# A routed feed-forward kernel: the third and fourth tile of an expert's tokens as one pair of 256 tokens, other PSUM banks in the branches, branch hints later in a tile, and the pair's code last in its branch

## The chip, the cores and the metric

The program runs on one core of one Trainium2 chip. The metric is the device time of one execution in microseconds; shown is the median of several. A core has five engines with their own instruction queues: TensorE (PE, matmuls; PEld are its weight loads), VectorE (DVE), ScalarE (ACT), GpSimd (POOL) and SyncE (SP, which here only starts transfers). They meet by semaphores.

## The reference

Three stages follow each other. Local and global attention of 4 batches and 8 heads gives 2176 tokens of width 512. Each goes through a feed-forward layer (512 to 2048, squared ReLU, back to 512). Then comes the stage that is changed here, a layer of 8 experts:

```python
skip_score = x @ w_skip
do_compute = skip_score > 0
out = x.copy()
xc = x[do_compute]
logits = xc @ w_gate
e_idx = np.argmax(logits, axis=1)
gate_w = ...                        # the softmax probability of the chosen expert
for e in range(E):
    mask = e_idx == e
    h = np.maximum(xc[mask] @ w1[e], 0.0)       # 512 to 1024
    y[mask] = gate_w[mask, None] * (h @ w2[e])  # 1024 to 512
out[do_compute] = xc + y
```

How many tokens an expert gets depends on the data: the program learns it while it runs.

## The kernel before

The order of all work is written out by hand. For the experts it is plain program order: expert 0 to 7, and within an expert tiles of 128 tokens, tile 0 always and each later one in a runtime branch, nested: `more(e, j)` is an `If` on the expert's count of tokens that holds tile `j` and, inside, `more(e, j + 1)`; after tile 4 comes a loop. An engine that skips such an arm runs a few instructions in its place that wait until the engine's own work is done and then raise the semaphores by what the arm would have raised them. They have the line of the `If` (L1166). L1151 marks a branch hint: each engine is told early which way the branch will go.

Products are made at near float32 precision: each operand is split into a high and a low part, and a product is three matmuls (high by high, high by low, low by high). A tile (`expert_tile`) gathers its 128 token rows by an indirect transfer (L863, into `xg`), transposes them on PE (`etr`, four 128x128 transposes), and splits the result on ACT and DVE (`prepare`, `xp`). The first product (L889 to L891) has the tokens as the stationary operand and 512 columns of w1 as the moving one, so its result `eh` has tokens on the partitions; ACT applies ReLU (L894), PE transposes `er` back (`ertr`, four transposes for each half of the 1024 columns), ACT and DVE split that (`ehl`), and the second product (L904 to L906) adds up `y` over 8 blocks. DVE multiplies by the gate and adds the token (`eo`, L927), and POOL scatters the rows to the output (L931).

A tile is a generator of nine units u = 0 to 8. Beside them the program places the gathers of later tiles, the transposes of the next tile (u = 5 in tile `j` for tile `j + 1`; in tile 0 also u = 6 for the next expert), and, in tile 0 only, the conversion of an expert's weights: eight pieces of 512 KB, each cast to its high part on ACT (L828, `e26h` for piece 26, which is expert 3's third) and subtracted for the low part on DVE (L834, `e26l`). The pieces of an expert are converted from u = 3 of the tile before into its own tile 0. The first results `eh` of all tiles go to the PSUM tag "h" with two banks; the tags "s" and "o" with one bank each served the attention and are free here.

Of the kernel before, what the change touches and what calls it, by code (L numbers as in the profile page):

```python
# [53 lines left out]
def attention_ffn_routed_experts(  # L54
# [25 lines left out]
    P = 128  # L80
# [96 lines left out]
    def split(hi, lo, src, lo_engine=None):  # L177

        nc.scalar.copy(hi, src)  # L179
        (lo_engine or nc.vector).tensor_tensor(out=lo, in0=src, in1=hi.bitcast(F32), op=ALU.subtract)  # L180
# [625 lines left out]
    AHEAD = {2: ((2, 0),), 3: ((1, 1),)}  # L806
    PARTS_AT = {0: (0, 1), 1: (2,), 2: (3,), 3: (4,), 4: (5,), 5: (6,), 6: (7,)}
    U0, U1 = 6, 5

    def fetch_expert(n, queue=nc.sync):  # L810
        e, i = divmod(n, NPE)
# [42 lines left out]
                xps[chain, z] = sb(tag, bufs, [P, 2, KD, P], f"xp{chain}_{z}", F32R)  # L854

    def gathered(e, j):
        return xgs[(0, e % 3) if j == 0 else (1, e % 2) if j % 2 else (2, 0)]

    def prepared(e, j):
        return xps[(0, e % 2) if j == 0 else (1, 0) if j == 1 else (2, j % 2)]  # L860

    def gather(e, j, gi):
        nc.gpsimd.indirect_dma_start(  # L863
# [4 lines left out]
    def prepare(e, j):  # L868
        tr = pair(f"etr_{e}_{j}")
        transposes(tr, gathered(e, j))  # L870
        x = prepared(e, j)
        split(x[:, 0], x[:, 1], tr)

    def expert_tile(e, j, si):

        name = f"{e}_{j}"
        xg, p = gathered(e, j), prepared(e, j)
        hs, rs = [None] * 2, [None] * 2
        hl = sb("kT", 1, [P, NPAIR, S], f"ehl_{name}").rearrange("p a s -> p (a s)")[:, 0:2 * KE * P].bitcast(F32R)
        gh, gl = (hl[:, z * KE * P:(z + 1) * KE * P].rearrange("p (f k) -> p f k", f=KE) for z in range(2))  # L880
        y = ps.tile([P, DM], F32, tag="x2", bufs=2, name=f"y_{name}")

        def first(fb, k0, k1):
            if k0 == 0:
                hs[fb] = ps.tile([P, 512], F32, tag="h", bufs=2, name=f"eh_{name}_{fb}")
            h = hs[fb]
            for k in range(k0, k1):
                wh, wl = ew[e, 1, (fb, k)]
                nc.tensor.matmul(h, lhsT=p[:, 0, k, :], rhs=wh, start=(k == 0), stop=False)  # L889
                nc.tensor.matmul(h, lhsT=p[:, 0, k, :], rhs=wl, start=False, stop=False)  # L890
                nc.tensor.matmul(h, lhsT=p[:, 1, k, :], rhs=wh, start=False, stop=(k == KD - 1))  # L891
            if k1 == KD:
                rs[fb] = sb("sm", 2, [P, S], f"er_{name}_{fb}")[:, 0:512]
                nc.scalar.activation(rs[fb], h, AF.Relu)  # L894

        def turn(fb):
            tr = pair(f"ertr_{name}_{fb}")
            transposes(tr, rs[fb])
            split(gh[:, 4 * fb:4 * fb + 4, :], gl[:, 4 * fb:4 * fb + 4, :], tr)

        def second(f0, f1):
            for f in range(f0, f1):
                wh, wl = ew[e, 2, f]
# [12 lines left out]
        yield  # L916
        second(0, 2)
        turn(1)
        yield
        second(2, 4)  # L920
        yield
        second(4, 6)
        yield
        second(6, KE)
        yield
        o = sb("xt", 1, [P, 3 * BLK], f"eo_{name}")[:, 0:DM]
        nc.vector.scalar_tensor_tensor(  # L927
            out=o, in0=y, scalar=xg[:, DM:DM + 1], in1=xg[:, 0:DM], op0=ALU.mult, op1=ALU.add
        )
        yield  # L930
        nc.gpsimd.indirect_dma_start(  # L931
            out=out, out_offset=bass.IndirectOffsetOnAxis(ap=si, axis=0), in_=o, in_offset=None,
            bounds_check=NTOK - 1, oob_is_err=False,
        )

    rest = []

    def prepare_rest():
# [6 lines left out]
    def rest_tile(si):  # L945

        e, x, fw = E - 1, rest[0], F // NQ
        xg = gathered(e, 1)[0:SEG]
        raws = [est[e * NPE + i] for i in range(NPE)]
        h = ps.tile([P, 512], F32, tag="h", bufs=2, name="eh_rest")[:, 0:fw]  # L950
        for k in range(KD):
            for c in range(NQ):
                fb, at = divmod(c * fw, DM)
                nc.tensor.matmul(
                    h[SEG * c:SEG * (c + 1), :], lhsT=x[:, k, :],
                    rhs=raws[fb * (KD // 2) + k // 2][:, k % 2, at:at + fw],
                    start=(k == 0), stop=(k == KD - 1),
                )
        r = sb("sm", 2, [P, S], "er_rest")[:, 0:fw]
        nc.scalar.activation(r, h, AF.Relu)  # L960
        tr = pair("ertr_rest")
        nz = fw // P
# [13 lines left out]
        o = sb("xt", 1, [P, 3 * BLK], "eo_rest")[0:SEG, 0:DM]  # L976
        for d in range(NQ):
            cols = slice(d * P, (d + 1) * P)
            nc.vector.scalar_tensor_tensor(
                out=o[:, cols], in0=y[SEG * d:SEG * (d + 1), :], scalar=xg[:, DM:DM + 1], in1=xg[:, cols],  # L980
                op0=ALU.mult, op1=ALU.add,
            )
        nc.gpsimd.indirect_dma_start(  # L983
            out=out, out_offset=bass.IndirectOffsetOnAxis(ap=si[0:SEG], axis=0), in_=o, in_offset=None,
            bounds_check=NTOK - 1, oob_is_err=False,
        )
# [4 lines left out]
    with tc.manual_schedule():  # L991
# [103 lines left out]
        def slot(idx, e, j):  # L1095
            c = e * TPE + j
            return idx[:, c:c + 1]
# [46 lines left out]
                gather(n, j, slot(gidx, n, j))  # L1144

        def least(e, j):
            return j * P + (SEG if (e, j) == (E - 1, 1) else 0)

        def hint(e, j):

            tc.mark_branch_hint_location(f"more{e}_{j}", hint=n_tok[e] > least(e, j), engines=ENGINES)  # L1151

        def more(e, j):

            if j == UNROLL:
                with tc.For_i(UNROLL, (n_tok[e] + (P - 1)) // P, 1) as it:
                    gi = sb("gi", 2, [P, 1], f"gi{e}", I32)
                    nc.vector.tensor_copy(gi, gidx[:, bass.ds(it + e * TPE, 1)])
                    si = sb("si", 2, [P, 1], f"si{e}", I32)
                    nc.vector.tensor_copy(si, sidx[:, bass.ds(it + e * TPE, 1)])  # L1160
                    gather(e, UNROLL, gi)
                    prepare(e, UNROLL)
                    for _ in expert_tile(e, UNROLL, si):
                        pass
                return
            with tc.If(n_tok[e] > least(e, j), label=f"more{e}_{j}") as branch:  # L1166
                if j + 1 < UNROLL:
                    hint(e, j + 1)
                    gather(e, j + 1, slot(gidx, e, j + 1))
                for u, _ in enumerate(expert_tile(e, j, slot(sidx, e, j))):  # L1170
                    if u == 5 and j + 1 < UNROLL:
                        prepare(e, j + 1)
                more(e, j + 1)
            if least(e, j) > j * P:
                with branch.Else():
                    with tc.If(n_tok[e] > j * P):
                        rest_tile(slot(sidx, e, j))

        n_tok = None
        for e in range(E):  # L1180
            for u, _ in enumerate(expert_tile(e, 0, slot(sidx, e, 0)) if e else ()):
                if u == 0:
                    hint(e, 1)
                if u == U1:
                    prepare(e, 1)
                    if e == E - 1:
                        prepare_rest()
                if u == U0 and e + 1 < E:
                    prepare(e + 1, 0)
                work(e, u)  # L1190
# [39 lines left out]
```

## Time and profile before

| | |
|---|---|
| runs | 741.7, 740.62, 739.76 us; median 740.62 us |
| the profiled execution | 740.43 us, of which the span from first to last instruction is 738.6 us |
| PE busy over the span | 708.3 us (96%), 7509 matmuls |
| DVE, ACT, POOL busy | 420.2, 393.3, 168.5 us |
| mean granted TensorE clock | 0.988 of 2.4 GHz |

The experts' tiles stand from about 557 us to the end. Experts 0 and 3 have several full tiles, expert 7 one and a small rest, the others one tile each. Matmuls overlap, so the distance between the starts of two of them is the time that one costs, not its duration; a start that is later than its predecessor's by more than that distance is a wait. In the rows "[0.27 <-ACTq L1166]" is the idle time before an instruction and what ended it; a q behind an engine's name means its instruction queue, not its data path.

### The profile page before, as it was taken

To read this page: it belongs to the slowest core of one execution; us is meant where nothing else is said; L and a number is where in the kernel's file an instruction comes from. 1 tells how busy PE (TensorE), PEld (TensorE's weight loads), DVE (VectorE), ACT (ScalarE), POOL (GpSimd) and SP (SyncE) were. 2 spreads that over 40 slices of the span, in tenths; PEclk is the share of its full clock that TensorE was granted. 3 is DMA by queue.
4 is the path that set the end of the run, shared out by engine and by line. 5 is a ranking of instruction groups with operands and counts; after the bars stand their busy time and mean duration, and the time that the engine had idled before them with its cause. 6 is when DMAs were issued, how large, how long until landed. Compare 5 with 4: busy or idle time off the path is not lost. (4 is left out here: it accounts for less than half of the span.)

```text
span 738.6 us, 18687 instructions
## 1 busy us (share of the span) xinstructions
PE 708.3 (96%) x7509; PEld 588.1 (80%) x7509; DVE 420.2 (57%) x1077; ACT 393.3 (53%) x968; POOL 168.5 (23%) x213
## 2 busy tenths in 40 slices
PE   6689999999999999999999999999999999999996
PEld 4466677889888888888888988888878777887774
DVE  1889955853652463556165265342576279615993
ACT  5767567665544553534555454343354368515781
POOL 5000144461121121212112111122132222222121
PEclk8799999999999999999999999999999999999999
DMA  9999461073146114063501204100475779615920
GB/s 269 249 296 302 173 152 36 19 182 47 35 107 145 48 37 105 2 133 77 123 31 37 70 14 143 59 28 3 163 210 171 270 239 339 241 46 180 337 71 17
DMA packets 119462, 96.07 MB, mean 130 GB/s; under 512 B 84997, under 2 KB 92165, under 8 KB 119348
## 3 DMA queue, kind: packets, MB, share of 16 engines
q1 hardware_dynamic: 108304, 71.01, 35.0%
q10 hardware_dynamic: 8292, 15.48, 6.4%
q0 software_dynamic: 2752, 8.07, 3.4%
q8 instruction: 71, 1.16, 0.7%
q14 instruction: 43, 0.35, 0.2%
HBM read 82.28 MB, written 13.18 MB: 129 GB/s over the span
## 5 line engine op out<-in xcount | busy, mean ns | idle before, releaser
L180 POOL TENSOR_TENSOR gl<-g,gh 128x256 fp32r<-128x256 f32 x107 | 79.7, 745 | 302.2 <-ACT gh L179 154.7
L696 PE MATMUL h<-xh,w_in 128*128 128x256 f32 x464 | 134.7, 290 | 0.7 <-ACT xh L179 0.7
L697 PE MATMUL h<-xl,w_in 128*128 128x256 f32 x464 | 129.5, 279 | 0.3 <-DVE xl L180 0.3
L698 PE MATMUL h<-xh,w_in 128*128 128x256 f32 x464 | 129.7, 279 | 0.0
L721 PE MATMUL acc<-w_out,gh 128*128 128x512 f32 x232 | 97.7, 421 | 1.5 <-ACT gh L179 1.5
L723 PE MATMUL acc<-w_out,gl 128*128 128x512 f32 x232 | 91.9, 396 | 0.2
L722 PE MATMUL acc<-w_out,gh 128*128 128x512 f32 x232 | 91.6, 395 | 0.0
L696 PEld LDWEIGHTS h<-xh,w_in 128*128 128x128 f32 x464 | 87.0, 188 | 4.2 <-ACT xh L179 0.9
L700 ACT ACTIVATE g<-h 128x256 f32<-128x256 f32 x128 | 48.8, 382 | 76.7 <-PE h L698 43.3
L697 PEld LDWEIGHTS h<-xl,w_in 128*128 128x128 f32 x464 | 87.3, 188 | 2.7 <-DVE xl L180 0.5
L698 PEld LDWEIGHTS h<-xh,w_in 128*128 128x128 f32 x464 | 87.0, 188 | 0.0
L429 ACT ACTIVATE sm<-sm,mx 128x128 f32<-128x128 f32 x120 | 46.7, 391 | 49.5 <-DVE mx L427 49.5
L737 DVE TENSOR_TENSOR g<-h,g 128x256 f32<-128x256 f32 x53 | 22.2, 420 | 85.4 <-ACT g L700 85.3
L179 ACT CAST gh<-g 128x256 fp32r<-128x256 f32 x116 | 47.2, 407 | 42.2 <-DVE g L737 40.2
L723 PEld LDWEIGHTS acc<-w_out,gl 128*128 128x128 f32 x232 | 43.6, 188 | 12.0 <-POOL gl L180 1.4
L721 PEld LDWEIGHTS acc<-w_out,gh 128*128 128x128 f32 x232 | 43.6, 188 | 8.5 <-ACT gh L179 1.9
L722 PEld LDWEIGHTS acc<-w_out,gh 128*128 128x128 f32 x232 | 43.8, 189 | 5.6
L180 DVE TENSOR_TENSOR ehl<-ertr,ehl 128x512 fp32r<-128x512 f32 x26 | 18.0, 691 | 38.8 <-ACT ehl L179 38.8
L863 POOL DMA_INDIRECT xg<-x2d,slots x19 | 23.6, 1243 | 47.6 <-DVE ehl L180 15.0
L422 DVE TENSOR_TENSOR sm<-sc,mask 128x512 f32<-128x512 f32 x30 | 20.6, 687 | 23.8 <-PE sc L409 23.1
L894 ACT ACTIVATE er<-eh 128x512 f32<-128x512 f32 x26 | 15.6, 600 | 34.6 <-PE eh L891 31.1
L251 POOL TENSOR_TENSOR w_in<-st_raw_in,w_in 128x512 fp32r<-128x512 f32 x10 | 13.0, 1307 | 81.2 <-ACT w_in L247 81.2
(724 smaller groups left out, 1584.0 us busy)
## 6 DMA issues: line engine op xcount, KB each, us to landing
st_e<-in_moe_w_dram SPq DMA_DIRECT2D x52, 512.0 KB, 6.0
vr<-in_v_l_dram SPq DMA_DIRECT2D x49, 192.0 KB, 4.0
st_raw_in<-in_moe_w_in_dram SPq DMA_DIRECT2D x16, 512.0 KB, 7.4
st_raw_out<-in_moe_w_out_dram SPq DMA_DIRECT2D x16, 512.0 KB, 5.6
st_e<-in_moe_w_dram ACTq DMA_DIRECT2D x12, 512.0 KB, 4.8
x2d<-x ACTq DMA_DIRECT2D x19, 256.5 KB, 4.4
st_gv<-in_v_l_dram SPq DMA_DIRECT2D x8, 512.0 KB, 4.1
out_dram<-x ACTq DMA_DIRECT2D x16, 256.0 KB, 4.1
```

Of the source, the lines that this page charges most:

```text
L179: nc.scalar.copy(hi, src)
L180: (lo_engine or nc.vector).tensor_tensor(out=lo, in0=src, in1=hi.bitcast(F32), op=ALU.subtract)
L429: nc.scalar.activation(sm[:, hh, :], sm[:, hh, :], AF.Exp, bias=mx[:, hh:hh + 1], scale=SCALE, accum_out=osum[:, 2 * hh + g:2 * hh + g + 1],)
L696: nc.tensor.matmul(h, lhsT=wh, rhs=xh[:, k, :], start=(k == 0), stop=False)
L697: nc.tensor.matmul(h, lhsT=wh, rhs=xl[:, k, :], start=False, stop=False)
L698: nc.tensor.matmul(h, lhsT=wl, rhs=xh[:, k, :], start=False, stop=(k == KD - 1))
L700: nc.scalar.activation(g, h, AF.Relu)
L721: nc.tensor.matmul(acc[z], lhsT=gh[:, c], rhs=wh, start=first_one, stop=False)
L722: nc.tensor.matmul(acc[z], lhsT=gh[:, c], rhs=wl, start=False, stop=False)
L723: nc.tensor.matmul(acc[z], lhsT=gl[:, c], rhs=wh, start=False, stop=last_one)
L737: nc.vector.tensor_tensor(out=square, in0=h, in1=g, op=ALU.mult)
L863: nc.gpsimd.indirect_dma_start(out=gathered(e, j), out_offset=None, in_=x2d, in_offset=bass.IndirectOffsetOnAxis(ap=gi, axis=0), bounds_ch ...
```

## The change

It has four parts.

1. For experts 1 to 7 a third and fourth tile become one pair of 256 tokens (`expert_pair`) if the expert has more than 384 tokens. Its first product has w1 as the stationary operand (128 columns at a time) and the 256 tokens as the moving one, so its result has the hidden units on the partitions already and needs no transposing back; ACT writes the high part with the ReLU, DVE the low part in one operation. The second product is as before, for two blocks of tokens. Both tiles' gathers are issued at the start of tile 1, and their transposes stand at u = 5 and u = 6 of tile 1; the split parts lie side by side (`joint`). With 257 to 384 tokens the third tile runs alone as before.
2. `eh` of every tile inside a branch goes to the tags "s" and "o" instead of "h" (`inner`).
3. A branch hint stands at u = 4 of the tile before the branch (`HINT`), where it stood at u = 0 or ahead of the tile; in the pair it stands after its fifth block.
4. The pair's arm is the `Else` of `more_two`, and so the last in the code; a fifth tile's gather and transposes are made in its own arm.

```diff
+    HINT = 4
     def gathered(e, j):
-        return xgs[(0, e % 3) if j == 0 else (1, e % 2) if j % 2 else (2, 0)]
+        if j == 3 and e:
+            return xgs[0, e % 3]
+        return xgs[(0, e % 3) if j == 0 else (1, e % 2) if j % 2 or (j == 4 and e) else (2, 0)]
+
+    def joint():
+        return [xps[2, z].rearrange("p a k c -> p (a k c)").rearrange("p (k c) -> p k c", k=KD) for z in range(2)]
...
+    def inner(in_arm, z, name):
+        tag = ("s", "o")[z % 2] if in_arm else "h"
+        return ps.tile([P, 512], F32, tag=tag, bufs=BANKS[tag], name=name)
...
-                hs[fb] = ps.tile([P, 512], F32, tag="h", bufs=2, name=f"eh_{name}_{fb}")
+                hs[fb] = inner(j > (not e), fb, f"eh_{name}_{fb}")
...
+    def expert_pair(e, sis):
+
+        ph, pl = joint()
+        ys, gs = [], {}
+
+        def first(f):
+            fb, c = divmod(f * P, DM)
+            cols = slice(c, c + P)
+            h = inner(True, f, f"eph_{e}_{f}")[:, 0:BLK]
+            for k in range(KD):
+                wh, wl = ew[e, 1, (fb, k)]
+                nc.tensor.matmul(h, lhsT=wh[:, cols], rhs=ph[:, k, :], start=(k == 0), stop=False)
+                nc.tensor.matmul(h, lhsT=wh[:, cols], rhs=pl[:, k, :], start=False, stop=False)
+                nc.tensor.matmul(h, lhsT=wl[:, cols], rhs=ph[:, k, :], start=False, stop=(k == KD - 1))
+            gh, gl = gs[f] = [sb(n, 3, [P, BLK], f"e{n}_{e}_{f}", F32R) for n in ("gh", "gl")]
+            nc.scalar.activation(gh, h, AF.Relu)
+            nc.vector.scalar_tensor_tensor(
+                out=gl, in0=h, scalar=0.0, in1=gh.bitcast(F32), op0=ALU.max, op1=ALU.subtract
+            )
+
+        def second(f):
...
+            for z in range(2):
+                c = slice(z * P, (z + 1) * P)
+                nc.tensor.matmul(ys[z], lhsT=gh[:, c], rhs=wh, start=(f == 0), stop=False)
+                nc.tensor.matmul(ys[z], lhsT=gh[:, c], rhs=wl, start=False, stop=False)
+                nc.tensor.matmul(ys[z], lhsT=gl[:, c], rhs=wh, start=False, stop=(f == KE - 1))
+
+        first(0)
+        for f in range(KE):
+            if f + 1 < KE:
+                first(f + 1)
+            second(f)
+            yield f
...
-                if j + 1 < UNROLL:
-                    hint(e, j + 1)
-                    gather(e, j + 1, slot(gidx, e, j + 1))
+                if e and j == 4:
+                    gather(e, j, slot(gidx, e, j))
+                    prepare(e, j)
+                    following = ()
+                else:
+                    following = (2, 3) if e else range(j + 1, UNROLL)[:1]
+                for z in following:
+                    gather(e, z, slot(gidx, e, z))
                 for u, _ in enumerate(expert_tile(e, j, slot(sidx, e, j))):
-                    if u == 5 and j + 1 < UNROLL:
-                        prepare(e, j + 1)
-                more(e, j + 1)
+                    if u == HINT and following:
+                        hint(e, j + 1)
+                    if 5 <= u < 5 + len(following):
+                        prepare(e, following[u - 5])
+                more(e, j + 1) if j != 1 else more_two(e)
...
+        def more_two(e):
+
+            with tc.If(n_tok[e] <= least(e, 2), label=f"more{e}_2") as branch:
+                with tc.If(n_tok[e] > 2 * P):
+                    for _ in expert_tile(e, 2, slot(sidx, e, 2)):
+                        pass
+            with branch.Else():
+                for f in expert_pair(e, [slot(sidx, e, z) for z in (2, 3)]):
+                    if f == HINT:
+                        hint(e, 4)
+                more(e, 4)
...
             for u, _ in enumerate(expert_tile(e, 0, slot(sidx, e, 0)) if e else ()):
-                if u == 0:
+                if u == HINT:
                     hint(e, 1)
```

Three places show what moves. The first is PE in expert 3 where hidden units are made for the second product. Before, in the third tile (`eh_3_2`), the first half is done and transposed back:

```order
L890 MATMUL eh_3_2_1_10471<-e26l_10204,xp2_0_8023 128x512
L891 MATMUL eh_3_2_1_10471<-e26h_9661,xp2_0_8023 128x512
L276 MATMUL ertr_3_2_0_10478<-ident_70,er_3_2_0_10469 128x128 [waits Activation_49]
L276 MATMUL ertr_3_2_0_10478<-ident_70,er_3_2_0_10469 128x128 x3
L889 MATMUL eh_3_2_1_10471<-e27h_10202,xp2_0_8023 128x512
L890 MATMUL eh_3_2_1_10471<-e27l_10210,xp2_0_8023 128x512
```

Now, in the pair (`eph` is the first product's result, `egh` and `egl` its split parts, `yp` the second product's):

```order
L960 MATMUL eph_3_1_10751<-xp2_1_8024,e25h_9748 128x256
L961 MATMUL eph_3_1_10751<-xp2_0_8023,e25l_9769 128x256
L975 MATMUL yp_3_0_10768<-e28h_10405,egh_3_0_10747 128x512 [waits Activation_49]
L976 MATMUL yp_3_0_10768<-e28l_10421,egh_3_0_10747 128x512
L977 MATMUL yp_3_0_10768<-e28h_10405,egl_3_0_10748 128x512 [waits DVE_49]
L975 MATMUL yp_3_1_10769<-e28h_10405,egh_3_0_10747 128x512
L976 MATMUL yp_3_1_10769<-e28l_10421,egh_3_0_10747 128x512
L977 MATMUL yp_3_1_10769<-e28h_10405,egl_3_0_10748 128x512
L959 MATMUL eph_3_2_10776<-xp2_0_8023,e24h_9729 128x256
```

The transposes are gone, and the 256-column matmuls of a block alternate with the second product of the block before it. The second place is PE at the end of expert 3's tile 1. Before (`y_3_1` is that tile's second product, `eh_3_2` the first product of the third tile):

```order
L904 MATMUL y_3_1_10354<-e31h_10259,ehl_3_1_10353 128x512
L905 MATMUL y_3_1_10354<-e31l_10283,ehl_3_1_10353 128x512
L906 MATMUL y_3_1_10354<-e31h_10259,ehl_3_1_10353 128x512
L1166 COMPARE_AND_BRANCH
L1151 REGISTER_ALU
L1225 BRANCH_PREFETCH_HINT
L889 MATMUL eh_3_2_0_10456<-e24h_9623,xp2_0_8023 128x512 [waits Activation_49]
L890 MATMUL eh_3_2_0_10456<-e24l_9644,xp2_0_8023 128x512
```

Now (`etr_3_3` are the fourth tile's token transposes):

```order
L918 MATMUL y_3_1_10554<-e30h_10439,ehl_3_1_10553 128x512
L276 MATMUL etr_3_3_10639<-ident_70,xg0_0_7727 128x128 [waits DMASW4_49,PE_49]
L276 MATMUL etr_3_3_10639<-ident_70,xg0_0_7727 128x128 x3
L916 MATMUL y_3_1_10554<-e31h_10456,ehl_3_1_10553 128x512
L917 MATMUL y_3_1_10554<-e31l_10495,ehl_3_1_10553 128x512
L918 MATMUL y_3_1_10554<-e31h_10456,ehl_3_1_10553 128x512
L916 MATMUL y_3_1_10554<-e31h_10456,ehl_3_1_10553 128x512
L917 MATMUL y_3_1_10554<-e31l_10495,ehl_3_1_10553 128x512
L918 MATMUL y_3_1_10554<-e31h_10456,ehl_3_1_10553 128x512
L1252 COMPARE_AND_BRANCH
```

A group of four transposes came in ahead of the last six matmuls, and the hint that followed the branch has gone from there. The third place is DVE where expert 3 begins: the skipped arm's instruction, then the low parts of expert 3's third, fourth and fifth weight piece. Before:

```order
L1166 UNCONDITIONAL_BRANCH [waits DVE_49] x4
L1151 REGISTER_ALU
L1225 BRANCH_PREFETCH_HINT
L834 TENSOR_TENSOR e26l_10204<-st_e26_8924,e26h_9661 128x1024 [waits DMAHW2_49,PE_49,Activation_49]
L834 TENSOR_TENSOR e27l_10210<-st_e27_8941,e27h_10202 128x1024 [waits DMAHW3_49,Activation_49]
L834 TENSOR_TENSOR e28l_10224<-st_e28_8963,e28h_10208 128x1024 [waits DMAHW4_49,Activation_49]
L180 TENSOR_TENSOR ehl_3_0_10176<-ertr_3_0_0_10233,ehl_3_0_10176 128x512 [waits Activation_49]
```

Now:

```order
L1230 UNCONDITIONAL_BRANCH [waits DVE_49] x2
L835 TENSOR_TENSOR e26l_10401<-st_e26_8909,e26h_9767 128x1024 [waits DMAHW2_49,PE_49,Activation_49]
L835 TENSOR_TENSOR e27l_10407<-st_e27_8926,e27h_10399 128x1024 [waits DMAHW3_49,Activation_49]
L835 TENSOR_TENSOR e28l_10421<-st_e28_8963,e28h_10405 128x1024 [waits DMAHW4_49,Activation_49]
L180 TENSOR_TENSOR ehl_3_0_10388<-ertr_3_0_0_10430,ehl_3_0_10388 128x512 [waits Activation_49]
```

The register operation and the hint between the skipped arm and `e26l` are gone from this place; they stand later in the tile.

## Rows read from the trace of the kernel before

**Rows 1.** Windows, third tile of expert 3: stretch, length, busy (instructions), clock, DMA

```profile
647.50:660.00 12.50, 12.50 (x62) 10.24 (x61) 2.83 (x4) 2.96 (x5) 2.06 (x2) 1.00 0.13 42
```

**Rows 2.** Instructions by tile name: durations min/median/max ns, first and last start

```profile
L889 PE MATMUL eh<-e24h,xp x8: 389/393/498, 622.1 to 660.7; 128*128 128x512 f32 x8
```

**Rows 3.** Timeline of PE, third and fourth tile of expert 3: start us, duration us

```profile
647.58 0.40 PE L889 MATMUL eh<-e24h,xp 128*128 128x512 f32 x1
...
651.78 0.60 PE L276 MATMUL ertr<-ident,er 128*128 128x128 f32 x4
...
652.46 0.40 PE L890 MATMUL eh<-e27l,xp 128*128 128x512 f32 x1
...
672.23 0.39 PE L906 MATMUL y<-e31h,ehl 128*128 128x512 f32 x1
673.06 0.50 PE L889 MATMUL eh<-e32h,xp 128*128 128x512 f32 x1 [0.44 <-PEq L1166]
```

**Rows 4.** Timeline of PE in the dense feed-forward stage, 256-column matmuls

```profile
399.94 0.28 PE L698 MATMUL h<-xh,w_in 128*128 128x256 f32 x1
...
400.62 0.28 PE L698 MATMUL h<-xh,w_in 128*128 128x256 f32 x1
...
409.63 0.28 PE L696 MATMUL h<-xh,w_in 128*128 128x256 f32 x1
...
411.04 0.40 PE L721 MATMUL acc<-w_out,gh 128*128 128x512 f32 x1
...
411.98 0.39 PE L722 MATMUL acc<-w_out,gh 128*128 128x512 f32 x1
```

**Rows 5.** Timeline of PE's weight loads, same stage

```profile
402.63 0.19 PEld L697 LDWEIGHTS h<-xl,w_in 128*128 128x128 f32 x1
```

**Rows 6.** Timelines of PE and DVE, one tile's transposes and the end of their split

```profile
644.39 0.60 PE L276 MATMUL etr<-ident,xg 128*128 128x128 f32 x4
...
645.64 0.69 DVE L180 TENSOR_TENSOR xp<-etr,xp 128x512 fp32r<-128x512 f32 x1 [1.14 <-ACT xp L179]
```

**Rows 7.** The page's costliest groups, ACT and DVE on 128x256 from PSUM

```profile
L700 ACT ACTIVATE g<-h 128x256 f32<-128x256 f32 x128 | 48.8, 382 | 76.7 <-PE h L698 43.3
...
L737 DVE TENSOR_TENSOR g<-h,g 128x256 f32<-128x256 f32 x53 | 22.2, 420 | 85.4 <-ACT g L700 85.3
```

**Rows 8.** Timeline of POOL, the gather of expert 3's third tile

```profile
638.79 1.02 POOL L863 DMA_INDIRECT xg<-x2d,slots  x1 [0.31 <-issue]
```

**Rows 9.** Timeline of PE, end of expert 2 and begin of expert 3

```profile
621.47 0.40 PE L906 MATMUL y<-e23h,ehl 128*128 128x512 f32 x1
622.14 0.50 PE L889 MATMUL eh<-e24h,xp 128*128 128x512 f32 x1 [0.27 <-ACTq L1166]
...
625.04 0.40 PE L889 MATMUL eh<-e26h,xp 128*128 128x512 f32 x1
...
625.63 0.39 PE L891 MATMUL eh<-e26h,xp 128*128 128x512 f32 x1
```

**Rows 10.** Line 1166 there: the branch and the skipped arm's semaphore instructions, ns

```profile
L1166 PEldq COMPARE_BRANCH  x1: 352/352/352, 619.4 to 619.4; - x1
...
L1166 PEldq EVENT_SEMAPHORE  x1: 51/51/51, 621.9 to 621.9; - x1
...
L1166 ACTq EVENT_SEMAPHORE  x1: 17/17/17, 622.1 to 622.1; - x1
```

**Rows 11.** Timeline of DVE there

```profile
622.87 0.74 DVE L927 SCALAR_TENSOR_TENSOR eo<-y,xg 128x512 f32<-128x512 f32 x1
624.01 1.23 DVE L834 TENSOR_TENSOR e26l<-st_e,e26h 128x1024 fp32r<-128x1024 f32 x1 [0.40 <-DVEq L1166]
```

**Rows 12.** Waits from 594 to 727 us: total us, times, longest us

```profile
PE eh L889 <- ACTq L1166: 1.1, 4, 0.3
...
PEld eh L890 <- DVE e26l L834: 0.3, 1, 0.3
```

**Rows 13.** The page's queues: packets, MB, share of 16 engines' span

```profile
q8 instruction: 71, 1.16, 0.7%
```

More of the change, by code (lines that the diff above doesn't have):

```diff
@@ L856, in gathered @@
     def gathered(e, j):
-        return xgs[(0, e % 3) if j == 0 else (1, e % 2) if j % 2 else (2, 0)]
+        if j == 3 and e:
[3 more added lines that the diff above has]
+        return [xps[2, z].rearrange("p a k c -> p (a k c)").rearrange("p (k c) -> p k c", k=KD) for z in range(2)]
     def prepared(e, j):
-        return xps[(0, e % 2) if j == 0 else (1, 0) if j == 1 else (2, j % 2)]
+        if j > 1:
+            return [x[:, :, j % 2 * P:(j % 2 + 1) * P] for x in joint()]
+        x = xps[(0, e % 2) if j == 0 else (1, 0)]
+        return x[:, 0], x[:, 1]
     def gather(e, j, gi):
@@ L870, in prepare @@
         transposes(tr, gathered(e, j))
-        x = prepared(e, j)
-        split(x[:, 0], x[:, 1], tr)
+        split(*prepared(e, j), tr)
+    def inner(in_arm, z, name):
+        tag = ("s", "o")[z % 2] if in_arm else "h"
+        return ps.tile([P, 512], F32, tag=tag, bufs=BANKS[tag], name=name)
     def expert_tile(e, j, si):
         name = f"{e}_{j}"
-        xg, p = gathered(e, j), prepared(e, j)
+        xg, (ph, pl) = gathered(e, j), prepared(e, j)
         hs, rs = [None] * 2, [None] * 2
@@ L888, in first @@
                 wh, wl = ew[e, 1, (fb, k)]
-                nc.tensor.matmul(h, lhsT=p[:, 0, k, :], rhs=wh, start=(k == 0), stop=False)
-                nc.tensor.matmul(h, lhsT=p[:, 0, k, :], rhs=wl, start=False, stop=False)
-                nc.tensor.matmul(h, lhsT=p[:, 1, k, :], rhs=wh, start=False, stop=(k == KD - 1))
+                nc.tensor.matmul(h, lhsT=ph[:, k, :], rhs=wh, start=(k == 0), stop=False)
+                nc.tensor.matmul(h, lhsT=ph[:, k, :], rhs=wl, start=False, stop=False)
+                nc.tensor.matmul(h, lhsT=pl[:, k, :], rhs=wh, start=False, stop=(k == KD - 1))
             if k1 == KD:
@@ L934, in expert_tile @@
         )
+    def expert_pair(e, sis):
[16 more added lines that the diff above has]
+        def second(f):
+            gh, gl = gs.pop(f)
+            wh, wl = ew[e, 2, f]
+            if f == 0:
+                ys.extend(ps.tile([P, DM], F32, tag="x2", bufs=2, name=f"yp_{e}_{z}") for z in range(2))
+            for z in range(2):
[9 more added lines that the diff above has]
+            yield f
+        os = [sb("xt", 1, [P, 3 * BLK], f"eop_{e}_0")[:, 0:DM], sb("x2", 2, [P, ROW], f"eop_{e}_1")[:, 0:DM]]
+        for z in range(2):
+            xg = gathered(e, 2 + z)
+            nc.vector.scalar_tensor_tensor(
+                out=os[z], in0=ys[z], scalar=xg[:, DM:DM + 1], in1=xg[:, 0:DM], op0=ALU.mult, op1=ALU.add
+            )
+        for z in range(2):
+            nc.gpsimd.indirect_dma_start(
+                out=out, out_offset=bass.IndirectOffsetOnAxis(ap=sis[z], axis=0), in_=os[z], in_offset=None,
+                bounds_check=NTOK - 1, oob_is_err=False,
+            )
     rest = []
@@ L949, in rest_tile @@
         raws = [est[e * NPE + i] for i in range(NPE)]
-        h = ps.tile([P, 512], F32, tag="h", bufs=2, name="eh_rest")[:, 0:fw]
+        h = inner(True, 0, "eh_rest")[:, 0:fw]
         for k in range(KD):
@@ L1146, in least @@
         def least(e, j):
+            if e and j == 2:
+                return 3 * P
             return j * P + (SEG if (e, j) == (E - 1, 1) else 0)
         def hint(e, j):
-            tc.mark_branch_hint_location(f"more{e}_{j}", hint=n_tok[e] > least(e, j), engines=ENGINES)
+            taken = n_tok[e] <= least(e, j) if e and j == 2 else n_tok[e] > least(e, j)
+            tc.mark_branch_hint_location(f"more{e}_{j}", hint=taken, engines=ENGINES)
         def more(e, j):
```

## The prediction

> **What bounds the kernel now.** I read the windows over the experts' stage first, for which engine is full there, then PE's timeline tile by tile, then what PE waits for between tiles, and last the queue instructions at those waits. In the window on expert 3's third tile PE is busy in all of 12.50 us at the full clock (1.00 is the 2.4 GHz level), while DVE and ACT have 2.83 and 2.96 us of work and DMA is at 0.13 [rows 1]. So a microsecond of PE work saved there is a microsecond off the end, as long as nothing else arrives late. That expert 3 has four tiles is seen by its weight piece `e24h`, which stands eight times on one line, two blocks of k in each tile [rows 2]; it therefore has more than 384 tokens and the pair's arm runs. No other expert has that many tiles, so the pair runs once. Elsewhere PE loses time only where one expert ends and the next begins: into expert 3 the next matmul starts 0.67 us after the last, where 0.23 is the usual distance, and a second, smaller slip follows at the third weight piece [rows 9].
>
> **Part 1, the pair.** Before, the third and fourth tile take from 647.58 to 672.23, plus one distance of 0.23: 24.88 us [rows 3]. They hold 96 matmuls of 512 columns (each tile 2 x 4 x 3 and 8 x 3) and six groups of four transposes: two `ertr` in each tile, and one `etr` in each for the tile after it. A group costs 0.45 us: from 651.78 to 652.46 is 0.68, less one matmul of 0.23 [rows 3].
>
> The pair has 8 x 12 = 96 matmuls of 256 columns, 8 x 6 = 48 of 512 and no transposes. The dense stage runs these very shapes, in the same alternation: twelve 256-column matmuls from 409.63 to 411.04 are 0.1175 us each, and the 512-column ones behind them 0.235 (411.04 to 411.98, four) [rows 4]. So 96 x 0.1175 + 48 x 0.235 = 11.28 + 11.28 = 22.56 us. The same columns are streamed as before; what goes is transposing. A faster stretch of the dense stage has 0.1133 (399.94 to 400.62, six) [rows 4]; with both shapes in that proportion the pair takes 21.76.
>
> Each 256-column matmul needs a weight load of its own, and the loads take 0.19 us in the record [rows 5], longer than the matmuls' distance of 0.1175 [rows 4]; so they run alongside. The Trainium skill (TensorE: Matmul & The Clock Gate, section LDWEIGHTS) gives a load as columns divided by 1.2 in ns, 107 ns for 128, and its section on the back-to-back gap lets both operations set the spacing: were none of it hidden, 96 x 0.107 = 10.3 us would come on top and the pair would lose. The trace does not bear that out, since matmul and load together fit into 0.1175 here.
>
> Tile 1 now also transposes the fourth tile: one more group, 0.45 us. The split of that group ends late. A group that starts at T has its low part from DVE at T + 1.94 (645.64 + 0.69 - 644.39) [rows 6]; PE has 0.45 of transposes and six matmuls of 0.235 behind T, so its pair begins at T + 1.86, and the second matmul, the first to need the low part, wants its load at once. I charge 0.15 us; between 0 (its load was ready to slip in) and 0.3.
>
> The gather for the fourth tile starts 1.3 us behind that of the third at 638.79 [rows 8] (1.02 and 0.31 idle), and its transposes stand 1.8 us behind those at 644.39 [rows 6], which did not wait. So it is hidden; were it not, PE would wait for it in full. Inside the pair a block's second product comes one whole first product (1.41 us) after its own; ACT and DVE take 0.38 and 0.42 on this shape [rows 7], in all 0.8 plus some tenths of semaphores, so it is covered. Only the last block could be uncovered; the bound is 0.8 us. The pair's two outputs on DVE replace one at the end, but the first can be written while PE does the other half of the last block.
>
> Sum of part 1: 24.88 - 22.56 - 0.45 - 0.15 = 1.72 us saved; from 0.9 (the 0.8 uncovered) to 2.7 (the faster spacing, no stall).
>
> **Parts 2 and 3, the way into the next expert.** An engine that skips an arm waits for its own work and raises its semaphore. On PE that is at 621.9, on ACT, which has a weight cast to finish, at 622.1 [rows 10], and PE's next matmul at 622.14 is put down to ACT [rows 9, 12]. It waits for ACT because `eh` of tile 0 shares its banks with tiles in the skipped arm. With "s" and "o" for these, the last use of "h" is in the tile just done, and ACT's raise need not be awaited. PE's own stays. That is worth about 0.1 us by the two times; between 0 and 0.2.
>
> That alone gives nothing: 3 us on, PE waits for DVE's `e26l`. There 625.04 to 625.63 is 0.59 for two distances of 0.235, so 0.12 is lost [rows 9, 12]; PE coming 0.1 earlier would wait 0.1 longer. But `e26l` itself starts only 0.40 us after DVE was free [rows 11], with four queue steps in between: the raise, the register operation, the hint, a wait. The change takes two of them away from there. By half of 0.40, less the raise's own wait, I take 0.16 us; from 0 to 0.3. DVE was busy through the hint's new place, where its queue runs ahead of its data path, so I charge nothing there; if uncovered it costs the 0.16 back. So each such passage gains the smaller of 0.1 + 0.12 and 0.16, that is 0.16.
>
> Passages from one single-tile branch skip to the next tile 0 are those into experts 2, 3, 5, 6 and 7 (four are named so in the waits [rows 12], the fifth I take as like them): 5 x 0.16 = 0.8 us, from 0 to 1.1. Into expert 4 PE waits on its own queue [rows 3], as it does into expert 1, after a nested branch; these stay. Part 4 moves code only; it is a rival below.
>
> **Sum.** 1.72 + 0.8 = 2.5 us off the profiled execution's 740.43: 737.9. The runs' median lies 0.19 above that execution, which gives 738.1. I say 738.0.
>
> **Rivals.**
>
> *A: late code, slower.* PE makes eight jumps: into experts 1 to 7, over an arm a third longer than before, and a new one over the single third tile into the pair; each hint comes half a tile later. Against it: PE's queue reads the branch at 619.4 and is through in 0.35 us [rows 10], 1.95 us before the last matmul's slot ends at 621.7 [rows 9]; before, no jump stalled PE. A code packet takes 0.7% x 738.6 x 16 / 71 = 1.17 us [rows 13]. If a jump finds its code missing and needs one packet, it stays hidden; two in a row expose 0.4 us, 8 x 0.4 = 3.1, giving 741.0; three expose 1.55, giving 740.4 - 2.5 + 12.4 = 750.3. It decides, beyond 0.3% slower, from 2.5 us per miss. The Trainium skill (Runtime: NRT & Kernel Launch, section Instruction fetch mechanics) says that a taken branch out of the two-block window waits for a transfer of the target block; the trace shows jumps over this distance with the hint half a tile earlier and no stall. Chance 0.08, at 750.3.
>
> *B: the passages do not move.* DVE keeps its slot because something else in the row of four steps sets it, or the hint costs the same at its new place. Then the pair alone: 740.4 - 1.7 = 738.7. For it: in a tile 0 DVE goes from subtract to subtract with no gap [rows 11]. Against it: the 0.40 us idle there. Chance 0.20.
>
> *C: the pair waits on ACT or DVE.* 0.8 us uncovered: 737.9 + 0.8 = 738.7. Against it: 1.41 us of cover. Chance 0.10.
>
> *D: the pair runs at the faster spacing.* 21.76 instead of 22.56: 737.1, with no stall 737.0. For it: DVE and ACT are nearly idle there [rows 1]. Against it: the quiet third tile already ran its 512 columns at 0.233. Chance 0.10.
>
> *The pair is not run at all* (an expert with 385 or more tokens is missing): excluded by [rows 2].
>
> **How the numbers follow.** The forecast has 0.52 and its own range 737.2 to 738.8. A measurement of this kernel tells from no change what is over 0.3%, here 2.2 us, so the line is 738.4. Of the forecast's 0.52 I put 0.42 below it and 0.10 above; D adds 0.10 and B and C 0.03 to faster, the rest of B and C 0.27 to no change, A 0.08 to slower. Faster 0.55, the same 0.37, slower 0.08. The range for 8 in 10 goes from 736.7 (D with the passages at 1.1) to 739.8 (B and C together, and 0.3 for the run); A is left out.
>
> **What would show it.** In the profile after: two shapes at the pair's lines with starts 0.1175 and 0.235 apart and 22.5 us from its first matmul to its last; no transposes between; one short wait at its second matmul. Into experts 2, 3, 5, 6 and 7 PE's wait no longer put down to ACT's queue, and the slip at the third weight piece not larger. Expert 4's first matmul near 670.9 instead of 673.06, and the same tail behind expert 7. It would be wrong if waits for ACT or DVE stand inside the pair, if the passages still take 0.67 us, or if PE stands idle behind a branch for more than a microsecond.

## The result, and the profile after

The changed kernel takes 751.69 us (median of 6 runs, 747.16 to 752.6) where the kernel before takes 740.42; the ratio of the means is 1.0134, 95% interval 1.0101 to 1.0167. It is slower by 11 us (10 by the means), outside the forecast range. All ratios below are of means, and runs more than 1.5% above the fastest of their kernel (two, of one experiment) are left out of them. The profiled execution took 747.53 us with a span of 745.8; where the runs at 751 to 752.6 lose the rest was not traced.

The third tile of expert 0 starts 0.5 us later than before (its first matmul at 582.19, before at 581.72), and the spans differ by 7.2 us, so nearly all of the loss lies behind it. The time from one expert's first matmul to the next one's, in us, worked out from PE's timelines (expert 0 from its third tile on):

```
expert            0      1      2      3      4      5      6      7 to the end
before        13.40  13.45  13.57  50.92  13.45  13.56  13.57  24.96
after         13.40  14.05  15.61  50.45  14.75  15.11  15.33  24.91
difference     0.00   0.60   2.04  -0.47   1.30   1.55   1.76  -0.05
```

Expert 3, with the pair, is shorter. Five of the single-tile experts are longer (a passage counts for the expert that it leaves). PE's waits in the experts' stage of the changed kernel (total us, times, longest us) say for what; the row of before that answers to them is [rows 12]:

```profile
PE eh L901 <- PEq L1230: 7.6, 6, 2.3
...
PE eh L902 <- DVE e50l L835: 0.2, 1, 0.2
```

PEq is PE's own instruction queue: PE waits for nothing that another engine does. PE's timeline into expert 3, which answers to [rows 9]:

```profile
622.58 0.40 PE L918 MATMUL y<-e23h,ehl 128*128 128x512 f32 x1
625.25 0.77 PE L901 MATMUL eh<-e24h,xp 128*128 128x512 f32 x1 [2.27 <-PEq L1230]
625.81 0.63 PE L902 MATMUL eh<-e24l,xp 128*128 128x512 f32 x1
626.24 0.63 PE L903 MATMUL eh<-e24h,xp 128*128 128x512 f32 x1
```

2.67 us instead of 0.67 pass between two matmuls, and the next ones come 0.43 apart instead of 0.23. The branch is behind it. Its row and that of its hint, into expert 3 and then into expert 7 (duration in ns, then when it started); [rows 10] has 352 ns for the branch before:

```profile
L1308 PEldq BRANCH_PREFETCH_HINT  x1: 35/35/35, 617.0 to 617.0; - x1
L1230 PEldq COMPARE_BRANCH  x1: 4611/4611/4611, 620.5 to 620.5; - x1
...
L1308 PEldq BRANCH_PREFETCH_HINT  x1: 30/30/30, 714.7 to 714.7; - x1
L1230 PEldq COMPARE_BRANCH  x1: 627/627/627, 718.2 to 718.2; - x1
```

The hint stands 3.5 us ahead of the branch in both, and only one of them stalls. The windows around the two show the difference (length, busy us and count of PE, PE's loads, DVE, ACT, POOL, then granted clock, DMA share, GB/s):

```profile
617.00:625.00 8.00, 5.98 (x33) 4.62 (x31) 7.50 (x9) 6.22 (x8) 2.61 (x2) 1.00 0.98 345
...
714.00:720.00 6.00, 6.00 (x34) 4.98 (x33) 5.78 (x6) 5.21 (x9) 0.00 (x0) 1.00 0.09 24
...
625.20:628.40 3.20, 3.15 (x8) 2.52 (x9) 3.11 (x3) 1.04 (x1) 0.82 (x1) 0.51 0.88 298
```

Into expert 3 the weights for later experts fill the DMA queues (0.98); into expert 7 nothing is left to load (0.09). The last row is the stretch behind the stall: the granted clock is 0.51 there, the lower of its two levels, after PE had stood for some 2.3 us. The eight distances from 625.25 to 628.37 take 3.12 us instead of 1.88, so the stall costs 1.2 us more. A second such stretch (0.50, from 707.1 to 709.7) follows the stall into expert 6.

The trace's DMA records say when PE's code arrives. Its packets have 16 KB; these are the ones between a hint and the end of its branch:

```
                      hint     packets of 16 KB (start to end)       branch read  done
before, into 3       608.68    614.89-615.89                           619.36    619.71
after,  into 3       617.03    618.06-619.12  622.60-623.75            620.47    625.08
after,  into 5       682.89    687.68-688.77                           686.37    690.28
after,  into 7       714.74    716.01-717.34                           718.23    718.86
```

In all stalled jumps of the changed kernel the branch is done 1.3 to 1.6 us after a packet's end. On quiet queues the packet starts 1.3 to 1.5 us after the hint (into 7 and behind 7), into 1, 2, 3, 5 and 6 2.7 to 5.6 us. That the loads make this difference is argued here; the run without weight loads below tests it. Into expert 1 the branch takes 3.1 us too, but PE waits no longer there than before (0.45 us). The kernel before had up to 6.9 us between a hint and the next packet, too (686.62 to 693.48, into expert 6), but 10.7 us from a hint to its branch.

The pair itself came out as forecast. PE's timeline at its begin and end, which answers to [rows 3]:

```profile
652.42 0.28 PE L959 MATMUL eph<-xp,e24h 128*128 128x256 f32 x1
652.59 0.39 PE L960 MATMUL eph<-xp,e24h 128*128 128x256 f32 x1
652.82 0.28 PE L961 MATMUL eph<-xp,e24l 128*128 128x256 f32 x1
652.94 0.28 PE L959 MATMUL eph<-xp,e24h 128*128 128x256 f32 x1
...
674.86 0.40 PE L977 MATMUL yp<-e31h,egl 128*128 128x512 f32 x1
675.70 0.50 PE L901 MATMUL eh<-e32h,xp 128*128 128x512 f32 x1 [0.45 <-PEq L1230]
```

From 652.42 to 674.86 and one distance of 0.23 is 22.67 us. The first three starts show the wait for the low part: 0.40 for two distances of 0.1175, 0.16 lost.

### The profile page after: what moved, and what is told of

It is laid out like the page before. It is cut to its first block, busy times and chain, and to the rows that moved or that the text cites. A ratio compares the mean times of both kernels' runs of the same rounds, so it can differ in the third digit from the quotient of the medians.

```text
span 745.8 us, 18733 instructions
## 1 busy us (share of the span) xinstructions
PE 710.5 (95%) x7537; PEld 591.2 (79%) x7537; DVE 420.6 (56%) x1080; ACT 390.8 (52%) x967; POOL 167.0 (22%) x212
## 4 chain that ended last, share of the span: by engine, by line
PE 68%; DMA 14%; issue 10%; SPq 3%; POOL 2%; DVE 1%; ACT 1%; POOLq 1%; another core or an unknown queue 0%; ACTq 0%
PE h L696 7%; PE acc L721 7%; PE acc L723 7%; PE h L697 7%; PE h L698 7%; PE acc L722 7%; DMA xg<-x2d,slots 6%; DMA out_dram<-eo,slots 4%; PE acc L719 3%; PE h L693 3%; PE sc L409 3%; PE po L447 2%; PE ptr L438 2%; DMA out_dram<-eop,slots 2%; SPq L365 1%
## 5 line engine op out<-in xcount | busy, mean ns | idle before, releaser
L180 DVE TENSOR_TENSOR ehl<-ertr,ehl 128x512 fp32r<-128x512 f32 x22 | 15.2, 691 | 30.1 <-ACT ehl L179 30.1
L872 POOL DMA_INDIRECT xg<-x2d,slots x18 | 21.9, 1219 | 44.5 <-DVE slots L796 13.1
L906 ACT ACTIVATE er<-eh 128x512 f32<-128x512 f32 x22 | 13.2, 598 | 31.1 <-PE eh L903 27.6
```

## The experiments

Theory T: the late hints; a jump's code is asked for too late, and its transfer waits behind weight loads. Its rivals: R1, the longer arms make the jumps miss wherever the hint stands; R2, 3.5 us are too few even on quiet queues.

**Early hints.** The changed kernel with one number changed.

```
-    HINT = 4
+    HINT = 0
```

> The changed kernel with one number changed: the hints stand behind the tile's first six matmuls again (HINT = 0), everything else (pair, own banks, order of the arms) as changed. Theory T (the code of the jump's target is fetched from the hint on, its transfer waits behind the weight loads on the same DMA engines, and 5.8 us from the hint to the end of the last matmul are too few): PE has some 13 us again, so no passage waits on its own queue for more than 0.5 us. The sum of the prediction without the late hint then stands: 737.5 to 738.8 us. Rival R1 (the longer arms and the pair's place make the jumps miss, wherever the hint stands): 747 to 752 us. Rival R2 (a late hint is too late even on quiet DMA queues, loads play no part): 737.5 to 738.8, as T.

Measured: 745.67 us, ratio 1.0063 (1.0045 to 1.0081). Neither theory's number. PE's waits, then DVE's timeline and the rows of its queue at the jump into expert 6:

```profile
PE eh L902 <- DVE e50l L835: 3.8, 1, 3.8
...
PE eh L901 <- PEq L1230: 1.0, 2, 0.5
```

```profile
700.76 0.74 DVE L939 SCALAR_TENSOR_TENSOR eo<-y,xg 128x512 f32<-128x512 f32 x1
705.74 1.22 DVE L835 TENSOR_TENSOR e50l<-st_e,e50h 128x1024 fp32r<-128x1024 f32 x1 [4.23 <-DVEq L1230]
```

```profile
L1230 DVEq COMPARE_BRANCH  x1: 61/61/61, 699.8 to 699.8; - x1
L1230 DVEq EVENT_SEMAPHORE  x1: 21/21/21, 705.4 to 705.4; - x1
```

PE's own stalls are gone, as T says: what is left of PEq are the two jumps that the kernel before had as well. But DVE read its branch at 699.8, ended its work at 701.5, and executed the jump's target, a semaphore instruction that waits for that work alone, at 705.4. A packet of 8 KB ends at 703.77 in the DMA records, 1.6 us before. DVE waits for code too, once, into expert 6. The changed kernel has the same stall there (709.1, its work done at 705.35), nearly hidden behind PE's own.

**Late hints alone,** in the kernel before.

```
-                if u == 0:
+                if u == 4:
                     hint(e, 1)
```

(and in the nested tiles `hint(e, j + 1)` from ahead of the tile to `u == 4`)

> The kernel before with the hints alone moved to the second half of each tile (behind step 4, as in the changed kernel); no pair, shared banks. T: PE waits on its own queue by some 0.3, 0.7, 2.1, 1.5 and 1.9 us more at the five passages where weights are still loading, and may fall to half the clock behind the longest: 747 to 752 us, nearly none of it into experts 6's end and 7. R1: no jump is longer than before, so 740.4, within 0.5. R2: the same 747 to 752, but with stalls of like size at the last two passages too.

Measured: 748.89 us, 1.0082 (1.0047 to 1.0116), single runs from 741 to 757. Its waits, and its branches into expert 2 (weights loading) and into expert 7 (queues quiet):

```profile
PE eh L889 <- PEq L1166: 8.0, 6, 3.2
```

```profile
L1166 PEldq COMPARE_BRANCH  x1: 5542/5542/5542, 606.4 to 606.4; - x1
...
L1166 PEldq COMPARE_BRANCH  x1: 438/438/438, 719.5 to 719.5; - x1
```

No jump is longer here than before, so R1 falls as the cause of PE's stalls, and the last row speaks against R2.

**Hints in the middle.** `HINT = 2` in the changed kernel.

> The changed kernel with the hints behind step 2 of the tile (HINT = 2), some 9.3 us before the last matmul's end. T: before the change the code packets came 2.5 to 6.9 us after the hint, and the jump is done about 2.5 us behind that, in all 5 to 9.4 us; so at most one passage stalls, by some tenths: 737.5 to 739.5. R1: 747 to 752. R2: 737.5 to 739.5.

Measured: 746.79 us, 1.0084 (1.0063 to 1.0104). One PE stall, into expert 3 (branch 3.9 us, 1.6 us of wait), where one packet (616.83) came ahead of the one behind which the jump was done (622.71); and DVE's stall as with early hints, for which PE waits 3.9 us. For PE, T had allowed one stall of some tenths, and it was 1.6 us; the total missed mainly because of DVE.

**No weight loads,** late hints kept.

```
+    FULL, fixed = 20, []
...
+        if n >= FULL:
...
+            est[n] = fixed[0][:, None, :].to_broadcast([P, 2, DM])
+            return
         est[n] = stage(f"e{n}").rearrange("p (k f) -> p k f", k=2)
```

> The changed kernel with its late hints (HINT = 4), but from the 21st weight piece on nothing is loaded: these pieces are read from one small tile that holds a constant, so the experts from the second half of expert 2 on compute with wrong weights; every instruction on PE, ACT and DVE stays. T: with quiet DMA queues the packet comes 1.3 to 1.5 us after the hint, and the jump is done in 4 us, within the 5.8 us: no passage behind expert 1 waits on PE's queue for more than 0.3 us, and no stretch falls to half the clock: 736.5 to 738.8. R1 and R2: the stalls stay, 746 to 752.

Measured: 740.06 us, 0.9997 (0.9982 to 1.0012). PE's waits, and a window just behind the hint into expert 3 (hint 616.17, code packet 621.24 to 622.20, branch done 623.57):

```profile
PE eh L908 <- PEq L1237: 4.4, 4, 1.6
```

```profile
616.20:618.00 1.80, 1.80 (x12) 1.49 (x11) 1.59 (x3) 1.60 (x3) 0.84 (x1) 1.00 0.00 0
```

PE still waits 4.4 us on its queue (7.6 with the loads), the longest 1.6; no jump is followed by a stretch at half the clock. So T's number failed, and with it most of what T says of the loads: into experts 2, 3, 5 and 6 the packets start 3.4, 5.1, 4.5 and 4.5 us after the hint, where it was 4.3, 5.6, 4.8 and 5.3 with the loads, and into expert 7 3.4 instead of 1.3. Into expert 3 no packet at all moves in the DMA records for the first 3.0 us behind the hint. R2 is right in that late hints miss without loads too; what holds those packets back stays open. The run differs in one more thing: without the waits for the loads the trace has 23 fewer DVE instructions ahead of its jump into expert 6, and DVE's stall is not there.

**DVE's place, shifted.** Theory L: where DVE's code falls against its blocks decides its stall; rival D: something else at this passage. Early hints, and tiny memsets on DVE at the program's start, where it is idle until 8.85 us:

```
+        pad = const.tile([P, 8], F32, name="pad")
+        for _ in range(16):
+            nc.vector.memset(pad, 0.0)
```

> The changed kernel with early hints (HINT = 0) and 16 tiny extra memsets on DVE at the start of the program, which DVE has time for there; they shift all later DVE code by 16 instructions. The early hints alone left one stall: DVE stood 3.9 us at its jump into expert 6 with its own work done, and PE behind it 3.8 us and then at half the clock. Theory L (where DVE's code falls against its blocks decides this stall): shifted by 16, DVE has no wait of over 0.3 us at any of the seven jumps, PE none on e50l, and the time is 738.3 to 739.5. Rival D (something else at this passage holds DVE, such as a transfer or the longer arm): the 3.9 us stay, 745 to 746.

Measured: 739.18 us, 0.9984 (0.9969 to 0.9999). The 3.8 us are gone; 1.1 us stand at the next jump instead, with the DMA queues quiet (share 0.01 from 711.9 to 713.9):

```profile
PE eh L902 <- DVE e58l L835: 1.1, 1, 1.1
PE eh L901 <- PEq L1233: 0.9, 2, 0.4
```

**The same shift for the kernel before:** 20 memsets, nothing else.

> The kernel before, unchanged but for 20 tiny extra memsets on DVE at the start; they put DVE's branch behind expert 5 at the same place of its code, by count, as in the changed kernel. L: the kernel before now gets the stall too: DVE stands 3 to 5 us at its jump into expert 6, PE waits for e50l 2.5 to 4.5 us: 743 to 746. D: nothing changes, 740.4 within 0.7.

Measured: 743.6 us, 1.0049 (1.003 to 1.0068). DVE's and PE's timelines:

```profile
700.99 0.74 DVE L927 SCALAR_TENSOR_TENSOR eo<-y,xg 128x512 f32<-128x512 f32 x1
706.23 1.23 DVE L834 TENSOR_TENSOR e50l<-st_e,e50h 128x1024 fp32r<-128x1024 f32 x1 [4.50 <-DVEq L1169]
...
707.51 0.50 PE L890 MATMUL eh<-e50l,xp 128*128 128x512 f32 x1 [3.96 <-DVE e50l L834]
```

Twenty instructions that do nothing, 700 us earlier, give the kernel before the changed kernel's stall. L holds, D is out.

**Hints one step later than early, 16 memsets.** `HINT = 1`.

> As the first of this set, but with the hints one step later (HINT = 1, behind twelve matmuls), which takes DVE's hint and its register operation out from before the first piece that the next expert waits for. L with theory T: PE keeps 11 us from the hint to the jump, enough for the 5 to 9.4 us, so no stall; five passages of 13.56 us become 13.45: 737.6 to 739.0, and 0.3 to 0.6 less than the first of this set. D: 745 to 746. If 11 us are too few at one passage: 740 to 742.

Measured: 738.03 us, 0.9973 (0.996 to 0.9986), with 1.0 us left on `e58l`. This beats both kernels.

**Late hints, 16 memsets.**

> The changed kernel as it is (HINT = 4) with the 16 extra memsets on DVE. T and L: PE's five stalls from the late hints stay, some 6 to 8 us with the stretches at half the clock; DVE's stall goes, but it lay mostly beside PE's own at that passage: 745 to 750. Rival: if DVE's stall made nearly all of the loss, 739 to 742.

Measured: 748.44 us, 1.0118 (1.0076 to 1.016). PE's waits; the second, into expert 6, stands behind a branch of 4.6 us, though the view puts it down to ACT:

```profile
PE eh L901 <- PEq L1233: 5.1, 5, 3.2
PE eh L901 <- ACT e51h L829: 2.2, 1, 2.2
```

With three of the kernels above this makes a table of ratios: late hints 1.0134 without and 1.0118 with the shift, early ones 1.0063 and 0.9984. The late hints cost 0.7% without and 1.3% with the shift. The shift gains 0.8% with early hints; with late ones its 0.2% lies well inside the intervals, so beside PE's own stalls DVE's stall is not shown to cost anything.

**Eight memsets.** `HINT = 1`.

> The changed kernel with the hints behind twelve matmuls (HINT = 1) and 8 instead of 16 tiny memsets on DVE. With 16, DVE's stall at the jump into expert 6 had gone, but one of 1.0 us stood at the jump into expert 7 (PE on e58l). L: by count, with 8 each of DVE's branches stands where one without a stall stood in some run before, so no DVE wait over 0.3 us is left on PE's path: 736.8 to 738.0, some 1.0 us under the kernel with 16. Rival (the 1.0 us at expert 7 has another cause than the place of the code): it stays, 737.7 to 738.7.

Measured: 743.99 us, 1.0046 (1.0031 to 1.0061): DVE's stall into expert 6 is back (PE 3.9 us on `e50l`). The expectation went by the wrong property of the place.

**No hints at all,** `hint` returns at once; 9 memsets.

> The changed kernel with all hints left out, and 9 tiny memsets on DVE so that its branches fall on places that showed no stall. T: a jump's code is then asked for only when the branch is read, some 2.4 us before PE needs it, and comes 4 us later on quiet queues and 5 to 7 under weight loads: seven stalls of 1.5 to 4.5 us and stretches at half the clock: 750 to 762, slower than the changed kernel as it is only where the late hints still helped (its two quiet passages, by 1 to 1.5 us each). Rival (the hints do nothing, and only their instructions' places differ): 738 to 741.

Measured: 757.36 us, 1.0219 (1.0197 to 1.0241), and no DVE stall. PE's waits:

```profile
PE eh L901 <- PEq L1233: 14.7, 7, 4.3
PE eh_rest L1015 <- issue: 2.6, 2, 1.3
```

The packets that these jumps wait for start 0.9 to 4.0 us after the branch is read; with a hint, into expert 7 in the table above, the packet starts 2.2 us before. So a late hint is worth half of what an early one is: 757.4 without, 748.4 late, 739.2 early, all three without DVE's large stall. The Trainium skill (Runtime: NRT & Kernel Launch, section Instruction fetch mechanics) says that a taken branch whose target is outside a window of two blocks waits for a transfer. These rows agree, with 14.7 us for seven jumps.

**The kernel before with `HINT` at 1.**

> The kernel before with the hints alone moved behind twelve matmuls (HINT = 1): single tiles, shared banks. It parts the gain of the first of this set into the hint's place and the rest. T: no stall; the hint is out of DVE's row before the first piece waited for, so the slip of 0.12 us at the third piece goes in five passages; the wait for ACT's queue at the tile's first matmul stays: 739.4 to 740.2, so that pair and banks make 2 us of the difference to the first of this set. Rival (the hint's place alone makes the gain): 737.5 to 738.5.

Measured: 740.93 us, 1.0004 (0.9991 to 1.0016). By itself this place of the hint gains nothing that shows in the time.

**A rule for the place, tested twice.** `HINT = 1`, with 56 memsets at the start and 4 ahead of each of six dense blocks, and with 50 and 2; in the traces DVE's later instructions stand 79 and 61 places further on.

> The changed kernel with HINT = 1 and tiny memsets on DVE, 56 at the start and 4 before each of six dense blocks, that shift its later code by 79. Rule C, read from the earlier runs: instruction transfers of DVE's size are 8 KB, 128 instructions; if a boundary of these falls within an expert's own stretch of 24 instructions, between its landing and its next jump, that jump stalls. The runs put the boundary at a count of 89 to 96 (mod 128); with 79 only expert 3's stretch (78 to 102) holds it, and expert 3 does not jump there. So DVE has no wait of over 0.3 us at any jump, PE none for e50l or e58l, and the time is 736.5 to 738.0. Rival N (the place of the code matters, but not by this rule): a stall of 1 to 4 us at some jump, 738 to 744.

> As the other of this set, but shifted by 61, which puts the boundary into expert 2's stretch (83 to 107). Rule C: the stall of 3 to 4 us now stands at the jump into expert 3 (PE on e26l), where weights are loading, and none at the jumps into experts 6 and 7: 740 to 744. Rival N: no stall there, or one elsewhere.

Measured: 743.99 us, 1.0039 (1.0021 to 1.0057), and 737.46 us, 0.9967 (0.9952 to 0.9982). Rule C is wrong, in both. DVE and PE of the first, then PE's waits of the second:

```profile
624.86 0.74 DVE L939 SCALAR_TENSOR_TENSOR eo<-y,xg 128x512 f32<-128x512 f32 x1
629.29 1.23 DVE L835 TENSOR_TENSOR e26l<-st_e,e26h 128x1024 fp32r<-128x1024 f32 x1 [3.68 <-DVEq L1238]
...
630.57 0.79 PE L902 MATMUL eh<-e26l,xp 128*128 128x512 f32 x1 [3.28 <-DVE e26l L835]
```

```profile
PE eh L901 <- PEq L1238: 0.9, 2, 0.4
PE eh L901 <- ACT xp L179: 0.7, 1, 0.7
```

The stall moved to another jump, into expert 3, with one shift and vanished with the other. That the place decides is shown; which property of it does is open. The second kernel has no such stall and is the best of all: 3.1 us under the kernel before. Not all of that is the change's. Some 0.5 us lie behind expert 7, where PE's wait for `er_rest` is 0.6 us instead of 1.1; so it is in the kernel before with 20 memsets.

## Why the prediction was wrong

**The step that failed** is in parts 2 and 3: "DVE was busy through the hint's new place, where its queue runs ahead of its data path, so I charge nothing there". I costed the hint as one instruction on DVE's chain. What it is for, the transfer that it starts, was priced only in rival A, and there by a packet's duration alone: 1.17 us, "if a jump finds its code missing and needs one packet, it stays hidden". The runs put in its place, at the four jumps where PE stood: 4.3 to 5.6 us until the packet starts (3.4 to 5.1 without weight loads), some 1.1 for it and 1.4 until the branch is done; in all 6.7 to 8 us, where a late hint leaves 5.8 until PE has run dry. So PE stood for 0.87, 2.27, 1.56 and 1.96 us into experts 2, 3, 5 and 6, and lost 1.2 us more at the lower clock behind the second. Rival A named place and sign. That its 750.3 lies near the measured 751.69 is luck: it comes from three packets in a row at eight jumps, and the runs show one late packet at four, with 747.53 in the execution that was traced. Its chance of 0.08 rested on the packet's duration, without the time until it starts. "Before, no jump stalled PE" was no evidence for its price, since the hints before had 10.7 us. The trace of before held the distances that would have said so: 3.6, 6.2, 4.3 and 6.9 us from a hint to the next code packet behind it, into experts 2, 3, 5 and 6.

**DVE's stall** was in no step. I took the moved code for a matter of jump lengths on PE; that an added arm shifts where another engine's code falls, and that one jump of DVE's can then wait 4 us for a packet, was not weighed. It adds 0.2 us of PE's wait in the changed kernel's profile, where PE itself is late. The kernel with early hints it cost more than its gain (1.0063 against 0.9984).

**The pair** was right. 22.67 us against 22.56 and 0.15; the spacing of 0.1175 by that of the dense stage; no wait for ACT or DVE inside, so the rivals C and D of the prediction are out. In the kernel shifted by 61, without stalls, expert 3 takes 49.22 us (621.66 to 670.88) where 50.92 were, a saving of 1.70 against 1.72.

**The passages** came out smaller. With early hints PE's first matmul comes 0.55 us after the last one instead of 0.67, no longer behind ACT's queue. But DVE still starts the third weight piece 0.40 us after it was free, and the slip there, by the prediction's own measure (two distances less 0.47), is 0.27 instead of 0.12: from expert 2 to 3 it is 13.56 us where 13.57 were, which is rival B. With `HINT = 1` the 0.40 falls to 0.26, here in the kernel shifted by 61 and likewise in the kernel before with `HINT` at 1:

```profile
623.52 1.28 DVE L835 TENSOR_TENSOR e26l<-st_e,e26h 128x1024 fp32r<-128x1024 f32 x1 [0.26 <-DVEq L1238]
```

That is 0.14 of the 0.16 that I took, but the operation itself takes 1.28 us instead of 1.23 [rows 11], so a passage gains 0.09. With `HINT = 1` and no stall the five stretches from one expert's first matmul to the next one's that hold these passages are 13.32, 13.48, 13.34, 13.48 and 13.47 us: 0.5 us in all against 0.8. So both terms are real, 2.2 us together. The version that keeps them is at 737.46, near the forecast 738.0, in part by the 0.5 us at the end that the sum did not have; the stalls that the change put on top were not in the sum either.

## What to carry to other kernels

A branch hint is the start of a transfer, not only an instruction: give it the whole time that code takes to arrive, here up to 8 us, and read that time from the code packets in the trace before moving it. Quiet DMA queues alone were no promise of a short one here. After a change of code ahead of or inside branches, look at every engine's first instruction behind its jumps; a stall there can come and go with a few instructions elsewhere, so a small gain or loss should be measured at more than one alignment before it is believed.

## What the runs showed of the hardware that was not expected

- DVE's jump into expert 6 stood 3.8 to 4.1 us with 0 or 8 added instructions in the changed kernel and with 20 in the kernel before, and not with 16 or 61 in the changed kernel or with none in the kernel before; 16 gave 1.1 to 1.3 us at the next jump, and 79 gave 3.5 us at one three experts earlier. ACT's jumps into these experts never stalled (0.03 us from its work's end).
- With no weight loads a code packet started 5.1 us after its hint, though no packet moved on any DMA queue for the first 3.0 us of that.
- In the changed kernel the granted clock fell to its lower level behind PE's waits of 2.27 and 1.96 us, not behind those of 0.87 and 1.56; behind the second it fell only 1.3 us after PE had started again (705.56 to 706.87).
- Late hints go with a wide spread: the kernel before with them took from 741 to 757 us in nine runs; the kernel shifted by 61 from 736 to 741 in twelve.
